# TensorE instead of DMA for the first transposes of an attention and mixture-of-experts kernel

## The chip, the core and the metric

The kernel runs on one core of a Trainium2 chip. The metric is device time in microseconds, the median of several runs. The core's engines have one queue each, worked in order: TensorE (PE in the profile; its weight loads PEld), VectorE (DVE), ScalarE (ACT), GpSimd (POOL) and SyncE (SP), which issues nearly all DMAs.

## The reference

Block-causal attention over 4 batches and 8 heads of 576 tokens, then a dense two-layer network with ELU over all 2304 tokens, then a second network with eight experts, of which every token that is not skipped takes one:

```python
def _attn_ref(q, k, v):
    scores = scale * np.matmul(q, k.transpose(0, 1, 3, 2))
    scores = np.where(block_i >= block_j, scores, -1000000000.0)   # blocks of 64
    attn = np.exp(scores - np.max(scores, axis=-1, keepdims=True))
    attn = attn / (np.sum(attn, axis=-1, keepdims=True) + 1e-09)
    return np.matmul(attn, v)
def _moe_ref(x, w_in, w_out):                    # 512 -> 2048 -> 512
    h = x @ w_in
    g = np.where(h > 0.0, h, np.exp(np.minimum(h, 0.0)) - 1.0)
    return g @ w_out
def _moe2_ref(x, w_skip, w_gate, w1, w2):        # per token: skip, or one expert
    h = np.maximum(xc[mask] @ w1[e], 0.0)
    y[mask] = gate_w[mask, None] * (h @ w2[e])
```

## The kernel before, in words

The 2304 tokens are nine chunks of 256 (`CT`). Attention feeds them: batch by batch, in groups of 64-token blocks (group 0 of batch 0 is blocks 0 to 3), for each group all four head pairs p, for each pair the blocks i. Nearly all fp32 values are carried as two fp16 halves (high and low), which are multiplied as three or so products.

- `load_raw` (L651) loads 128 tokens (tile n) of q, k or v for all heads into `raw`, a ring of three buffers.
- `prep_k` (L658) splits k into halves on ScalarE and VectorE (tile k1) and transposes them by a DMA on SyncE into KT (name kt). `prep_q` (L668) does the same with q, in two arrangements, high-low and low-high (qq, the first and second half of its first axis), of which the second takes one more ScalarE and one more VectorE instruction; one DMA transpose makes both parts of QT (qt). `prep_v` (L682) splits v with a scale from the largest value of v, which `vmax` (L613: a square with sum on ScalarE over the tile vflat) and `vscale` (L619: the maximum over partitions with two small matmuls, named bm, and a few VectorE instructions) find.
- For each pair and block, `s_unit` (L696) makes the scores in PSUM (tag s, three buffers), `x_unit` (L714) the maximum on VectorE and the exponential with its sum on ScalarE (e32, three buffers), `h_unit` (L741) the high halves of the normalised exponentials, for two blocks at a time, on ScalarE, and `l_unit` (L776) the low halves on VectorE, then a DMA transpose on SyncE from ehl into et (tag et0 to et4 by the number of 128-key tiles; et0, et1 and et3 have one buffer, et2 and et4 two). `pv` (L791) multiplies et with v's halves (xps) and copies the result into xt, the input of a chunk.
- Chunks 0 and 1 are computed in fp32. `l1` (L826) multiplies xt with the converted w_in (twi), `l1a` makes the ELU (g), `l2` (L871) multiplies with the converted w_out (two). Each of 32 raw weight tiles (rw) is loaded by `raw_load` (L454) and put in its final form by three VectorE instructions in `conv` (L480); two make one f of the eight of a layer. Chunk 0 needs the attention of group 0 for all pairs; chunk 1 needs the rest of batch 0's blocks up to 7.
- From chunk 2 on both layers are fp16 matmuls with split weights; after the last chunk come the experts.

The order. The code doesn't issue instructions at once: `Recorder` (L32) records steps with their reads, writes and buffer rings, and `order` (L149) plays the program with priced steps (`cost`, L310, and fixed latencies LAT): at each point the engine that can begin first takes, among the steps that are ready, the one recorded first. The result is each engine's queue. Group 0 of batch 0 and what it needs are recorded with an advance of 300 places (`hot`, L1147, `rc.base`). A step can be given an earliest time in `rc.ready`. Attention is recorded by place: the scores of a unit at its place x, maximum and exponential at x+1, high halves at x+2, low halves and transpose at x+3, pv five places after the last unit. So the scores of later units stand between the steps of one unit.

In the trace nearly all recorded instructions have line L307 (the recording helper), so tiles tell them apart.

Of the kernel before, what the change touches and what calls it, by code (L numbers as in the profile page):

```python
# [9 lines left out]
F32 = mybir.dt.float32  # L10
F16 = mybir.dt.float16
BF16 = mybir.dt.bfloat16
I32 = mybir.dt.int32
AF = mybir.ActivationFunctionType
# [6 lines left out]
ET_BUFS = 1, 1, 2, 1, 2  # L21
# [246 lines left out]
def _count(ap):  # L268
    n = 1
    for _, c in ap:  # L270
        n *= c
    return n
# [15 lines left out]
class _Engine:  # L288
# [21 lines left out]
    def cost(self, op, k):  # L310
        e = self.e
        out = k["out"]
        if e == "sp":
            b = _count(out.ap) * mybir.dt.size(out.dtype)
            if op == "dma_start_transpose":
                return max(1.2, b / 290e3 + 0.35), b / 290e3
            run = min(a.ap[-1][1] * mybir.dt.size(a.dtype) for a in (out, k["in_"]))
            return 0.48, b / 360e3 * (2 if run < 512 else 1)
        n = _count(out.ap[1:])
        sb = all(x.space == bass.MemoryType.SB for x in (out, k.get("in_", out), k.get("in0", out)))  # L320
        if e == "pe":
            if op == "transpose":
                return 0.2, 0.0
            t = n / 2400.0 * (4 if k["lhsT"].dtype == F32 else 1)
            here = out.offset // out.ap[0][0]
            prev, self.rec.last_pe = self.rec.last_pe, here
            return (0.02 if prev == 0 and here == 64 and n < 400 else max(t, 0.01)), 0.0
        if e == "act":
            aps = any(hasattr(k.get(x), "tensor") for x in ("scale", "bias"))
            return (0.094 if sb else 0.051) + n * 0.833e-3 + 0.093 * (aps + ("accum_out" in k)), 0.0  # L330
        if e == "dve":
            if op == "tensor_reduce":
                n = _count(k["in_"].ap[1:])
            aps = any(hasattr(k.get(x), "tensor") for x in ("scalar", "scalar1", "scalar2"))
            x = 1.0
            if op in ("tensor_copy", "tensor_scalar") and sb:
                x = 0.5 if mybir.dt.size(k.get("in_", k.get("in0")).dtype) == 4 else 0.25
            return 0.069 + n * x / 960.0 + 0.061 * aps, 0.0
        if op == "indirect_dma_start":
            return 1.05, 2.0  # L340
        return 0.15, 0.0
# [3 lines left out]
def tile_kernel(ctx, tc, q, k, v, w_in, w_out, w_skip, w_gate, w1, w2, out):  # L345
    nc = tc.nc
    B, H, S, D = q.shape
# [12 lines left out]
    G = [[[0, 1, 2, 3], [4, 5, 6, 7], [8]] if b == 0 else [[0, 1, 2, 3], [4, 5, 6, 7, 8]] for b in range(B)]  # L360
# [5 lines left out]
    mo = ctx.enter_context(tc.tile_pool(name="mo", bufs=1))  # L366
    ps = ctx.enter_context(tc.tile_pool(name="ps", bufs=1, space=PSUM))

    rc = Recorder(nc)
    wp, sm, mo, ps = (rc.pool(p_) for p_ in (wp, sm, mo, ps))  # L370
# [3 lines left out]
    ident = const.tile([128, 128], F32)  # L374
# [14 lines left out]
    def newcol(n=1):  # L389
        c = ncol[0]  # L390
        ncol[0] += n
        return slice(c, c + n)
# [28 lines left out]
    def setup_consts():  # L421
        make_identity(nc, ident)
        nc.gpsimd.memset(ones16, 1.0)
        nc.gpsimd.affine_select(out=tri16, in_=ones16, pattern=[[1, 128]], compare_op=ALU.is_gt, fill=0.0, base=0, channel_multiplier=-1)
        for e in range(E):
            nc.gpsimd.memset(rev[:, e:e + 1], float(E - e))
            nc.gpsimd.memset(eR[:, e:e + 1], float(e * R))
        nc.gpsimd.iota(tokid, pattern=[[128, NT // 128]], base=-2048, channel_multiplier=1, allow_small_or_imprecise_dtypes=True)
        nc.vector.memset(carry, 0.0)

        nc.vector.memset(carry[:, 2:3], 64.0)
        for h in range(2):
            nc.gpsimd.memset(pm[64 * h:64 * h + 64, 1:2], float(h))
            nc.gpsimd.iota(pm[64 * h:64 * h + 64, 0:1], pattern=[[0, 1]], base=64, channel_multiplier=1, allow_small_or_imprecise_dtypes=True)
# [159 lines left out]

    at = ExitStack()
    ap = rc.pool(at.enter_context(tc.tile_pool(name="attn", bufs=1)))
    XT = {}

    def xt(c):
        if c not in XT:  # L600
            if c < 2:
                XT[c] = mo.tile([128, 4, CT], F32, tag="xt", bufs=3, name="xt")
            else:
                XT[c] = mo.tile([128, 4, 2, CT], F16, tag="xt", bufs=3, name="xt")
        return XT[c]

# [5 lines left out]
    def vmax(b):  # L612
        if "vmx" not in st:  # L613
            st["vmx"] = newcol(4)
        s = st["vmx"].start
        t = st.pop(("vf", b))
        rc.scalar.activation(out=t, in_=t, func=AF.Square, accum_out=col[:, s + b:s + b + 1])

    def vscale(i):  # L619
        s = st["vmx"].start  # L620
# [22 lines left out]
    KT = {}  # L643
    QT = {}
# [3 lines left out]
    def trows(n):  # L648
        return 128 if n < 4 else 64

    def load_raw(nm, b, n):  # L651
# [3 lines left out]
        rc.sync.dma_start(out=t[0:r], in_=src[b, :, n * 128:n * 128 + r, :].rearrange("h p d -> p h d"))  # L655
        RAW[nm, b, n] = t

    def prep_k(b, n):  # L658
        r = trows(n)
        raw = RAW.pop(("k", b, n))  # L660
        if n == 0:
            KT[b] = ap.tile([128, H, S], F16, tag=f"kt{b % 2}", bufs=1, name="kt")
        k1 = ap.tile([128, H, 2, D], F16, tag="k1", bufs=1, name="k1")
        rc.scalar.activation(out=k1[0:r, :, 0, :], in_=raw[0:r], func=AF.Copy, scale=0.25)
        rc.vector.scalar_tensor_tensor(out=k1[0:r, :, 1, :], in0=raw[0:r], scalar=0.25, in1=k1[0:r, :, 0, :], op0=ALU.mult, op1=ALU.subtract)
        rc.sync.dma_start_transpose(out=KT[b][:, :, n * 128:n * 128 + r], in_=k1[0:r].rearrange("p h a d -> p (h a d)"))

    def prep_q(b, n):  # L668
        r = trows(n)
        raw = RAW.pop(("q", b, n))  # L670

        qq = ap.tile([128, 2, H, 2, D], F16, tag="qq", bufs=2, name="qq")
        for a in range(2):
            rc.scalar.activation(out=qq[0:r, a, :, a, :], in_=raw[0:r], func=AF.Copy, scale=0.5)
        rc.vector.scalar_tensor_tensor(out=qq[0:r, 0, :, 1, :], in0=raw[0:r], scalar=0.5, in1=qq[0:r, 0, :, 0, :], op0=ALU.mult, op1=ALU.subtract)
        rc.vector.tensor_copy(qq[0:r, 1, :, 0, :], qq[0:r, 0, :, 1, :])
        full = n < 4
        t = ap.tile([128, 2, H, r], F16, tag="qt" if full else "qh", bufs=3 if full else 1, name="qt")
        rc.sync.dma_start_transpose(out=t.rearrange("p a h r -> p (a h) r"), in_=qq[0:r].rearrange("p e h a d -> p (e h a d)"))
        QT[b, n] = t  # L680

# [12 lines left out]
    ET = {}  # L694
# [19 lines left out]
    def x_unit(b, p, i):  # L714
        tl, parts, mx = UN[b, p, i]

        for m, t in enumerate(tl):
            rc.vector.tensor_reduce(out=mx[:, m:m + 1], in_=t, axis=AX.X, op=ALU.max, negate=True)
        bias = mx[:, 0:1]
        if len(tl) == 2:  # L720
            bias = mx[:, 2:3]
            rc.vector.tensor_tensor(out=bias, in0=mx[:, 0:1], in1=mx[:, 1:2], op=ALU.min)
        x, u = i // 2, i % 2
        if u == 0:
            SU[b, p, x] = sm.tile([128, 8], F32, tag="su", bufs=4, name="su")
        es = []
        for m, (a, e_) in enumerate(parts):
            e32 = ap.tile([128, 64 if m else 512], F32, tag=("e32", "e3x")[m], bufs=(3, 2)[m], name="e32")
            es.append(e32[:, 0:e_ - a])
            rc.scalar.activation(out=es[m], in_=tl[m], func=AF.Exp, bias=bias, accum_out=SU[b, p, x][:, u + 2 * m:u + 2 * m + 1])  # L730
        UN[b, p, i] = es
# [5 lines left out]
    def pair(i):  # L737

        return [] if i % 2 == 0 and i < 8 else [8] if i == 8 else [i - 1, i]
# [36 lines left out]
    def l_unit(b, p, i):  # L776
        us = pair(i)
        if not us:
            return
        x = i // 2  # L780
        su = SU.pop((b, p, x))
        for u in us:
            for src, dst in e_parts(b, p, u):
                rc.vector.scalar_tensor_tensor(out=dst[:, :, 1], in0=src, scalar=su[:, 6 + u % 2:7 + u % 2], in1=dst[:, :, 0], op0=ALU.mult, op1=ALU.subtract)
            UN.pop((b, p, u))
        hl = HP.pop((b, p, x))
        n, nk = hl.shape[1:3]
        et = ET[b, p, x] = ap.tile([128, n, 2 * nk, 128], F16, tag=f"et{x}", bufs=ET_BUFS[x], name="et")
        rc.sync.dma_start_transpose(out=et.rearrange("p u n c -> p (u n) c"), in_=hl.rearrange("p u n a c -> p (u n a c)"))

    def pv(b, p, g):  # L791
# [474 lines left out]
    load_raw("q", 0, 1)  # L1266
    vflat(0)
    setup_consts()
    prep_k(0, 0)
    prep_q(0, 0)  # L1270
    load_raw("v", 0, 0)
# [244 lines left out]
    for i in range(2):  # L1516
        t = wp.tile([128, 2, PW], F32, tag=f"wo{i + 4}", bufs=1, name=f"gp{i}")
# [295 lines left out]
```

## Time and profile before

| | us |
|---|---|
| median of 3 runs | 803.34 (802.21 to 807.96) |
| profiled execution | 801.38 |
| its span, first to last instruction | 799.7 |
| TensorE busy | 699.3 (87%) |
| VectorE busy | 585.4 (73%) |
| ScalarE busy | 526.9 (66%) |
| mean granted TensorE clock | 0.986 |

The span is measured by the profiler on the core; some 1.7 us of the execution lie outside it. A row of a timeline gives the start, the time until the last of its merged instructions ended, the engine, the operation with the tiles written and read, and, in brackets, the idle time ahead of it with what ended it. A row of waits says who waited for whom, in total, how often, and the longest. A matmul's duration covers its pipeline, so the durations of neighbours overlap; busy time counts overlapping time once.

### The profile page before, as it was taken

To read this page: it belongs to the slowest core of one execution; us is meant where nothing else is said; L and a number is where in the kernel's file an instruction comes from. 1 tells how busy PE (TensorE), PEld (TensorE's weight loads), DVE (VectorE), ACT (ScalarE), POOL (GpSimd) and SP (SyncE) were. 2 spreads that over 40 slices of the span, in tenths; PEclk is the share of its full clock that TensorE was granted. 3 is DMA by queue.
4 is the path that set the end of the run, shared out by engine and by line. 5 is a ranking of instruction groups with operands and counts; after the bars stand their busy time and mean duration, and the time that the engine had idled before them with its cause. 6 is when DMAs were issued, how large, how long until landed. Compare 5 with 4: busy or idle time off the path is not lost. (4 is left out here: it accounts for less than half of the span.)

```text
span 799.7 us, 18029 instructions
## 1 busy us (share of the span) xinstructions
PE 699.3 (87%) x6586; PEld 461.1 (58%) x6586; DVE 585.4 (73%) x1721; ACT 526.9 (66%) x1166; POOL 98.3 (12%) x185
## 2 busy tenths in 40 slices
PE   0349868999998998999999999999998848998995
PEld 0238524675465655556646667675766635776763
DVE  3866988887998888987789648997876513737810
ACT  4555655999896886886578537673665425868832
POOL 2000000001001100100100100101040432322112
PEclk9999999999999999999999999999999979999998
DMA  9999999976897799898276089271564699989322
GB/s 226 256 204 291 294 299 256 213 130 122 165 176 139 138 181 202 170 197 155 49 125 143 19 162 374 94 225 40 188 181 141 123 236 236 330 240 216 70 29 39
DMA packets 300437, 141.43 MB, mean 177 GB/s; under 512 B 269659, under 2 KB 277989, under 8 KB 299808
## 3 DMA queue, kind: packets, MB, share of 16 engines
q1 hardware_dynamic: 295568, 130.65, 72.7%
q0 software_dynamic: 4752, 9.33, 4.8%
q8 instruction: 60, 0.98, 0.5%
q14 instruction: 57, 0.47, 0.2%
HBM read 76.20 MB, written 13.41 MB: 112 GB/s over the span
## 5 line engine op out<-in xcount | busy, mean ns | idle before, releaser
L307 PE MATMUL h<-xt,win 128*128 128x256 f16 x1344 | 159.5, 274 | 1.4 <-DVE n L307 1.0
L307 PE MATMUL y<-wout,g 128*128 128x512 f16 x672 | 156.5, 380 | 0.0
L307 PEld LDWEIGHTS <-win 128*128 128x128 f16 x1344 | 128.2, 98 | 28.2 <-issue 5.0
L307 PEld LDWEIGHTS <-g 128*128 128x128 f16 x672 | 62.4, 98 | 70.6 <-issue 5.2
L307 ACT ACTIVATE ehl<-e,su 128x64 f16<-128x64 f32 (+4 forms) x208 | 86.2, 470 | 22.7 <-DVE su L307 9.1
L307 ACT ACTIVATE e<-s,mx 128x64 f32<-128x64 f32 (+7 forms) x160 | 78.5, 492 | 34.0 <-DVE mx L307 16.3
L307 DVE SCALAR_TENSOR_TENSOR ehl<-e,su,ehl 128x64 f16<-128x64 f32 (+4 forms) x208 | 85.9, 442 | 9.8 <-ACT ehl L307 9.4
L307 PE MATMUL s<-kt,qt 128*64 128x512 f16 (+7 forms) x640 | 64.7, 306 | 25.6 <-ACT e L307 14.6
L307 DVE TENSOR_REDUCE mx<-s 128x1 f32<-128x64 f32 (+7 forms) x160 | 70.1, 448 | 11.5 <-PE s L307 11.1
L307 PE MATMUL xps<-et,vt 128*64 128x128 f16 (+1 forms) x1440 | 49.7, 220 | 22.0 <-DMA et<-ehl 19.0
L307 POOL MEMSET ehl<- 128x128 f16 x80 | 16.3, 210 | 403.2 <-DMA et<-ehl 284.2
L307 PEld LDWEIGHTS <-vt 128*64 128x64 f16 x1440 | 41.5, 115 | 39.3 <-issue 23.2
L307 PE MATMUL h<-xt,twi 128*128 128x256 f32 x256 | 63.3, 403 | 0.9 <-DVE g L307 0.9
L307 PE MATMUL y<-two,g 128*128 128x512 f32 x128 | 61.7, 613 | 2.4 <-DVE two L307 2.4
L307 PEld LDWEIGHTS <-qt 128*64 128x64 f16 x640 | 28.8, 115 | 57.8 <-issue 40.8
L307 PEld LDWEIGHTS h<-xt,twi 128*128 128x128 f32 x256 | 50.1, 201 | 10.6 <-DVE g L307 1.3
L307 ACT ACTIVATE el<-h,col 128x512 f32<-128x512 f32 x56 | 38.2, 682 | 25.3 <-PE h L307 25.1
L307 PE MATMUL y<-p,hh 128*128 128x512 f16 x192 | 46.0, 393 | 9.5 <-ACT hh L307 9.1
L307 ACT ACTIVATE g<-el,col 128x512 f16<-128x512 f32 x56 | 40.1, 717 | 19.6 <-DVE el L307 19.4
L307 PEld LDWEIGHTS <-hh 128*128 128x128 f16 x288 | 27.7, 99 | 43.1 <-ACT hh L307 9.6
L1450 DVE SCALAR_TENSOR_TENSOR p<-p,n,p 128x1024 f16<-128x1024 f32 x37 | 47.3, 1282 | 5.1 <-ACT p L1449 5.0
L307 PEld LDWEIGHTS <-p 128*128 128x128 f16 x768 | 45.8, 98 | 8.2 <-issue 3.7
(209 smaller groups left out, 1176.1 us busy)
## 6 DMA issues: line engine op xcount, KB each, us to landing
p<-in_moe_w_dram SPq DMA_DIRECT2D x45, 512.0 KB, 6.6
rw<-in_moe_w_in_dram SPq DMA_DIRECT2D x16, 512.0 KB, 5.1
rw<-in_moe_w_out_dram SPq DMA_DIRECT2D x16, 512.0 KB, 7.4
pb<-in_moe_w_dram SPq DMA_DIRECT2D x14, 512.0 KB, 5.6
vflat<-in_v_dram SPq DMA_DIRECT2D x4, 1152.0 KB, 7.3
out_dram<-pay SPq DMA_DIRECT2D x18, 256.0 KB, 3.5
pay_d<-pay SPq DMA_DIRECT2D x18, 256.0 KB, 2.6
raw<-in_k_dram SPq DMA_DIRECT2D x16, 256.0 KB, 3.9
```

What stands on the lines that cost most here:

```text
L307: rec.call(e, time, lambda: getattr(self.real, op)(*args, **kw), reads, writes, dma)
L1450: rc.call("dve", 1.2, lambda: nc.vector.scalar_tensor_tensor(out=half(1), in0=raw.t, scalar=sc, in1=half(0), op0=ALU.mult, op1=ALU.subtrac ...
```

## The change

For tiles 0 and 1 of batch 0 (`early`), k and q are transposed by TensorE into PSUM, in fp16, and copied from there into KT and QT: by VectorE for k, by ScalarE for q. q's second arrangement is made by transposing the halves in the other order, so that the instructions that built it for these tiles go. For group 0 of batch 0 the normalised exponentials go the same way, copied by ScalarE for even pairs and by VectorE for odd ones; odd pairs use the rings et4 and et2. The exponentials of blocks 2 and 3 of batch 0 go into a ring named el, otherwise free at that time. The square of `vmax` gets an earliest time of 11.5 in the planner. The planner prices an fp16 transpose at 0.06. GpSimd copies the identity to fp16 once. All other transposes stay DMAs.

```diff
@@ cost
             if op == "transpose":
-                return 0.2, 0.0
+                return (0.2 if out.dtype == F32 else 0.06), 0.0
@@ vmax
         rc.scalar.activation(out=t, in_=t, func=AF.Square, accum_out=col[:, s + b:s + b + 1])
+        if b == 0:
+            rc.ready[len(rc.steps) - 1] = 11.5
@@ new
+    def early(b, n):
+        return b == 0 and n < 2
+
+    def turn(out, ins, tag, dve=False):
+        t = ps.tile([128, len(ins), 128], F16, tag=tag, bufs=2, name="tp")
+        for x, a in enumerate(ins):
+            if isinstance(a, tuple):
+                for h in range(2):
+                    rc.tensor.transpose(out=t[64 * h:64 * h + 64, x, :], in_=a[h], identity=ident16)
+            else:
+                rc.tensor.transpose(out=t[:, x, :], in_=a, identity=ident16)
+        if dve:
+            rc.vector.tensor_copy(out, t)
+        else:
+            rc.scalar.activation(out=out, in_=t, func=AF.Copy)
@@ prep_k
+        if early(b, n):
+            turn(KT[b][:, :, n * 128:n * 128 + r], [k1[0:r, h].rearrange("p a d -> p (a d)") for h in range(H)], "y", True)
+            return
         rc.sync.dma_start_transpose(out=KT[b][:, :, n * 128:n * 128 + r], in_=k1[0:r].rearrange("p h a d -> p (h a d)"))
@@ prep_q
-        for a in range(2):
+        for a in range(1 if early(b, n) else 2):
             rc.scalar.activation(out=qq[0:r, a, :, a, :], in_=raw[0:r], func=AF.Copy, scale=0.5)
         rc.vector.scalar_tensor_tensor(out=qq[0:r, 0, :, 1, :], in0=raw[0:r], scalar=0.5, in1=qq[0:r, 0, :, 0, :], op0=ALU.mult, op1=ALU.subtract)
+        if early(b, n):
+            turn(t[:, 0], [qq[:, 0, h].rearrange("p a d -> p (a d)") for h in range(H)], "h")
+            turn(t[:, 1], [(qq[:, 0, h, 1], qq[:, 0, h, 0]) for h in range(H)], "h")
+            QT[b, n] = t
+            return
         rc.vector.tensor_copy(qq[0:r, 1, :, 0, :], qq[0:r, 0, :, 1, :])
@@ x_unit
+            if b == 0 and i in (2, 3):
+                e32 = mo.tile([128, 512], F32, tag="el", bufs=2, name="e32")
+            else:
+                e32 = ap.tile([128, 64 if m else 512], F32, tag=("e32", "e3x")[m], bufs=(3, 2)[m], name="e32")
@@ l_unit
-        et = ET[b, p, x] = ap.tile([128, n, 2 * nk, 128], F16, tag=f"et{x}", bufs=ET_BUFS[x], name="et")
+        y = (4, 2)[x] if b == 0 and x < 2 and p % 2 else x
+        et = ET[b, p, x] = ap.tile([128, n, 2 * nk, 128], F16, tag=f"et{y}", bufs=ET_BUFS[y], name="et")
+        if b == 0 and i in G[0][0]:
+            hf = hl.rearrange("p u n a c -> p (u n a) c")
+            turn(et.rearrange("p u n c -> p (u n) c"), [hf[:, y] for y in range(2 * n * nk)], "h", p % 2 == 1)
+            return
         rc.sync.dma_start_transpose(out=et.rearrange("p u n c -> p (u n) c"), in_=hl.rearrange("p u n a c -> p (u n a c)"))
@@ setup
     setup_consts()
+    rc.gpsimd.tensor_copy(out=ident16, in_=ident)
```

## Rows read from the trace of the kernel before

**Rows 1.** Busy time by stage; columns as its first line says (x: instructions).

```profile
core 0: us, PE busy (x) PEld busy (x) DVE busy (x) ACT busy (x) POOL busy (x), PEclk, DMA share, GB/s
0.00:55.00 55.00, 13.48 (x151) 9.32 (x151) 35.83 (x110) 29.48 (x81) 4.83 (x41) 1.00 1.08 227
22.83:54.99 32.16, 12.21 (x136) 8.66 (x137) 26.10 (x79) 20.29 (x63) 0.00 (x0) 1.00 1.10 226
55.00:92.00 37.00, 34.80 (x162) 27.80 (x161) 27.51 (x58) 24.25 (x43) 0.20 (x1) 1.00 1.08 292
92.00:144.00 52.00, 42.38 (x263) 18.88 (x263) 45.48 (x109) 29.29 (x64) 1.44 (x7) 1.00 1.09 269
150.00:640.00 490.00, 469.88 (x4520) 306.56 (x4515) 400.32 (x1271) 347.32 (x796) 51.07 (x104) 0.99 0.71 153
```

**Rows 2.** Timeline of PE, 0 to 160 us: start, us, what, idle before.

```profile
13.77 0.53 PE L307 MATMUL s<-kt,qt 128*64 128x64 f16 x8
...
22.83 1.39 PE L307 MATMUL s<-kt,qt 128*64 128x192 f16 x12 [8.17 <-DMA qt<-qq]
...
54.99 16.76 PE L307 MATMUL h<-xt,twi 128*128 128x256 f32 x64
...
145.54 1.36 PE L307 MATMUL xps<-et,vt 128*64 128x128 f16 x42
```

**Rows 3.** Waits, 0 to 60 us: in total, times, longest.

```profile
PE bm L307 <- ACT vflat L307: 13.3, 1, 13.3
...
PE s L307 <- DMA qt<-qq: 10.7, 2, 8.2
PE xps L307 <- DMA et<-ehl: 10.6, 5, 2.9
```

**Rows 4.** Timeline of SyncE's DMA queue, 0 to 60 us.

```profile
7.12 4.44 SPq L307 DMA_TRANSPOSE qt<-qq  x1
11.60 0.58 SPq L307 DMA_DIRECT2D raw<-in_q_dram  x1
...
17.29 3.38 SPq L307 DMA_TRANSPOSE qt<-qq  x1
```

**Rows 5.** Timeline of PE, 636 to 670 us.

```profile
640.23 5.53 PE L307 MATMUL hp<-mxwo,p 128*128 128x128 f16 x96 [0.87 <-ACTq L1674]
```

**Rows 6.** Groups by shape, whole span: busy, mean ns, idle before.

```profile
L307 DVE TENSOR_REDUCE mx<-s 128x1 f32<-128x512 f32 x32 | 21.6, 679 | 0.0
...
L307 DVE TENSOR_REDUCE mx<-s 128x1 f32<-128x256 f32 x16 | 6.7, 416 | 0.3 <-PE s L307 0.3
...
L307 ACT ACTIVATE pay<-y 128x512 f32<-128x512 f32 x4 | 2.4, 590 | 0.0
...
L307 ACT ACTIVATE xt<-xps 128x256 f16<-128x256 f32 x4 | 1.5, 378 | 3.0 <-PE h L307 2.5 <-PE xps L307 0.4
```

**Rows 7.** Groups by shape, 0 to 60 us: busy, mean ns, idle before.

```profile
L307 DVE SCALAR_TENSOR_TENSOR twi<-rw,twi 128x512 int32<-128x512 int32 x16 | 10.9, 686 | 0.1
...
L307 ACT ACTIVATE qq<-raw 128x512 f16<-128x512 f32 x6 | 3.4, 621 | 0.7 <-DMA raw<-in_q_dram 0.6
L307 DVE TENSOR_SCALAR twi<-rw 128x512 int32<-128x512 int32 x8 | 3.4, 420 | 1.1 <-DMA rw<-in_moe_w_in_dram 1.1
...
L307 ACT ACTIVATE vflat<-vflat 128x2304 f32<-128x2304 f32 x1 | 2.1, 2122 | 4.4 <-DMA vflat<-in_v_dram 4.4
L307 DVE SCALAR_TENSOR_TENSOR qq<-raw,qq 128x512 f16<-128x512 f32 x3 | 2.1, 688 | 1.0 <-ACT qq L307 1.0
...
L307 DVE COPY qq<-qq 128x512 f16<-128x512 f16 x3 | 0.9, 291 | 0.1
```

**Rows 8.** Timeline of DVE, 4.5 to 14 us.

```profile
4.82 0.69 DVE L307 SCALAR_TENSOR_TENSOR k<-raw,k 128x512 f16<-128x512 f32 x1 [2.15 <-ACT k L307]
```

**Rows 9.** DMA issues, 0 to 60 us: KB each, median us to landing.

```profile
raw<-in_q_dram SPq DMA_DIRECT2D x4, 256.0 KB, 4.3
...
et<-ehl SPq DMA_TRANSPOSE x8, 4.2
```

**Rows 10.** Waits of DVE, 60 to 160 us.

```profile
DVE two L307 <- DMA rw<-in_moe_w_out_dram: 5.7, 5, 2.4
...
DVE twi L307 <- DMA rw<-in_moe_w_in_dram: 3.2, 2, 2.3
```

More of the change, by code (lines that the diff above doesn't have):

```diff
@@ L596, in tile_kernel @@
     ap = rc.pool(at.enter_context(tc.tile_pool(name="attn", bufs=1)))
+    ident16 = ap.tile([128, 128], F16, tag="id16", bufs=1, name="id16")
     XT = {}
@@ L672, in prep_q @@
         qq = ap.tile([128, 2, H, 2, D], F16, tag="qq", bufs=2, name="qq")
-        for a in range(2):
+        full = n < 4
+        t = ap.tile([128, 2, H, r], F16, tag="qt" if full else "qh", bufs=3 if full else 1, name="qt")
+        for a in range(1 if early(b, n) else 2):
             rc.scalar.activation(out=qq[0:r, a, :, a, :], in_=raw[0:r], func=AF.Copy, scale=0.5)
         rc.vector.scalar_tensor_tensor(out=qq[0:r, 0, :, 1, :], in0=raw[0:r], scalar=0.5, in1=qq[0:r, 0, :, 0, :], op0=ALU.mult, op1=ALU.subtract)
+        if early(b, n):
[3 more added lines that the diff above has]
+            return
         rc.vector.tensor_copy(qq[0:r, 1, :, 0, :], qq[0:r, 0, :, 1, :])
-        full = n < 4
-        t = ap.tile([128, 2, H, r], F16, tag="qt" if full else "qh", bufs=3 if full else 1, name="qt")
         rc.sync.dma_start_transpose(out=t.rearrange("p a h r -> p (a h) r"), in_=qq[0:r].rearrange("p e h a d -> p (e h a d)"))
@@ L727, in x_unit @@
         for m, (a, e_) in enumerate(parts):
-            e32 = ap.tile([128, 64 if m else 512], F32, tag=("e32", "e3x")[m], bufs=(3, 2)[m], name="e32")
+            if b == 0 and i in (2, 3):
+                e32 = mo.tile([128, 512], F32, tag="el", bufs=2, name="e32")
+            else:
+                e32 = ap.tile([128, 64 if m else 512], F32, tag=("e32", "e3x")[m], bufs=(3, 2)[m], name="e32")
             es.append(e32[:, 0:e_ - a])
```

## The prediction

> **What bounds the kernel now.** I read the busy time by stage first, then who waited for whom in the first 60 us, then the order of TensorE's matmuls and of SyncE's issues there, and last the durations of the kinds of instruction that the change adds or removes.
>
> The stages [rows 1]: until 55 us TensorE is busy 13.5 us of 55; from 55 to 92 it is busy 34.8 of 37; from 92 to 144, 42.4 of 52 while VectorE is busy 45.5 of 52 (87%); from 150 to 640, 469.9 of 490 (96%). So the first 55 us are a stretch of waiting before TensorE, the bound of all that follows, gets its work. Its first large work is the first layer of token chunk 0 (h<-xt,twi), which begins at 54.99 [rows 2]. This needs the attention of blocks 0 to 3 of batch 0 for all four head pairs. So the question is what sets 54.99, and whether a shift of it lives on.
>
> What sets it [rows 3]: in 0 to 60 us the matmuls of s wait 10.7 us for the DMA transposes that make qt (8.2 of them in one wait), and those of xps 10.6 us in five waits for the ones that make et. The first s ran at 13.77, the first s of the second 128 tokens at 22.83 [rows 2]. Between lies SyncE's queue [rows 4]: the load of q's second tile is issued only at 11.60, behind the transpose of qq that held the queue from 7.12 for 4.44 us, and its own transpose goes out at 17.29 and takes 3.38 us to issue.
>
> **The change part by part.** Twelve DMA transposes go: kt and qt of tiles 0 and 1, and et of two shapes for four pairs. TensorE gets 2x8 transposes for k, 2x(8+16) for q, 4x(4+8) for the exponentials: 112. No 128-column fp16 transpose stands in the trace; the nearest are the matmuls with 128x128 weights and 128 columns, 96 in 5.53 us, 0.058 us each, weight loads hidden [rows 5]. The whole is 6.5 us. The first 64 sit where TensorE is idle anyway. Were they four times as long, the 24 of one q tile would put some 4 us on the start; at nothing they would save 1.4.
>
> Evictions from PSUM. On ScalarE a plain copy of 256 columns took 0.378 us and of 512 0.590 [rows 6], so 0.21 per 256 and 1.03 for 1024. On VectorE no copy out of PSUM is shown; reductions out of PSUM took 0.416 for 256 and 0.679 for 512 [rows 6], so 0.68 for 512 and 1.20 for 1024. From below the bound is the fp16 copy within SBUF, 0.291 for 512 [rows 7], 0.5 for 1024; I take 1.20, since the reductions read the memory that the copy reads. VectorE gains 2x1.20 for k and 2x(0.68+1.20) for the exponentials of the odd pairs, and loses two copies of 0.29: +5.6 us (+2.0 from below). ScalarE gains 4x1.03 for q and 2x(0.59+1.03) for the even pairs, and loses two conversions of 0.62: +6.1 us.
>
> One rule bears on the size. The Trainium skill (VectorE: DVE Perf Modes, "Why PSUM operands drop a tier") allows a copy with a PSUM operand up to twice the basic rate, and only fp32 the basic one; an fp16 copy of 1024 would then be an estimated 0.6 us, VectorE's gain 2.5 us, and the sum below some 1.5 us better. No row here shows an fp16 read of PSUM.
>
> The start. The raw tiles have three buffers, so q's second load waits until VectorE is done with the first k tile (4.82+0.69=5.5 [rows 8]) and no longer for two transposes. It goes out at 5.6 and lands 4.3 us later [rows 9], 9.9. Then ScalarE 0.62 and VectorE 0.69 [rows 7], 11.2; eight transposes 0.46; eviction 1.03, while the other sixteen run; second eviction, 13.9; s at 14. The square of vflat (2.12 us [rows 7]) is told to be due at 11.5 and may stand in ScalarE's queue before these evictions; the other end is 16.5. I take 15 against 22.83: 7.8 us gained. With the square moved, ScalarE no longer meets it before the second k tile; the wait for its sum (13.3 us, alone in the first 14 us [rows 3]) held no s. v's split, which the first xps needs, comes some 2 us behind the square; the first et needs maximum, exponential, split, transpose and eviction after its s and is later than that.
>
> The four pairs. From 22.83 to 54.99 is 32.2 us, with VectorE busy 26.1 and ScalarE 20.3 [rows 1]. Six conversions of weights lie in it, each three instructions, on average (10.9+3.4)/8=1.8 us [rows 7]: 10.8 us that can move. Each of the eight et transposes is 4.2 us from issue to landing [rows 9]; in its place stand 0.23 or 0.46 us of transposes and 0.6 to 1.2 of eviction, so 2.5 to 3.5 us less per hand-over, of which only the 10.6 us that TensorE waited can be won. What is late next is VectorE: 26.1 less 10.8 is 15.3, with the odd pairs' evictions 3.8 it is 19.1 without any conversion, and ScalarE 20.3+3.2=23.5. Some of either (the first units of blocks 4 and 5, the tiles that they need) can wait until later. The ends: 22 us (all conversions pushed out, ScalarE nearly full) and 32 (conversions stay between). I take 27, which wins half of the waits for et, 5.2 us. Chunk 0 begins at 15+27=42 instead of 55: 13 us.
>
> et gets two more buffers for odd pairs, and the exponentials of units 2 and 3 a ring of their own; both only take waits away, and I price them at nothing beyond the 27. GpSimd's copy of the identity stands behind 4.8 us of its own work, all it has before 55 [rows 1]; it may come a microsecond after the first k tile, which the 15 leaves room for. The et evictions take the PSUM buffers named h, which chunk 0 first needs after the last of them.
>
> What is given back. In front of 55 eight conversions were done, by 42 it will be about five; the first layer eats two per 4.2 us of TensorE (16.8 us for four f [rows 2]). From 55 to 144 VectorE was busy 27.5+45.5=73.0 of 89 [rows 1]; with three conversions more, 78.4 of 89, 88%, which is the share it reached in 92 to 144 while TensorE waited for it. So the length of this stretch should nearly hold. Ends: nothing, or three conversions and VectorE's new 5.6 us in full, 11. I take 3, a little over a quarter. DMA doesn't tighten it: the removed transposes carry 3.1 MB (two of 0.26, two of 0.52, four each of 0.13 and 0.26), 14 us at the 227 GB/s of that stretch [rows 1]. SyncE loses twelve issues and keeps the loads that stood behind them, and these only come sooner.
>
> A rule speaks against this change: the Trainium skill (Advanced Engine Details and Errata, "X-Bar Transpose (TRN2)") says that transpose DMAs are as fast as regular ones, 350 to 400 GB/s. At that rate an estimated 8 us of DMA time would be freed. The rows speak of latency, 4.2 us per et, not of rate, and the sum is the same by either.
>
> After 144 the shift is carried: 96% of TensorE's time from 150 to 640 is busy [rows 1], and weight loads there follow freed buffers, not a clock.
>
> **Sum.** 55 to 42 is -13, given back 3: -10 us. The profiled execution took 801.38 (span 799.7 and 1.7 around it): 791.4. It lies 2.0 under the median of 803.34, so for a median I say 793.3. A measurement tells about 1% (8 us) from no change.
>
> **Rivals.** (a) VectorE takes it back: the conversions missing at 42 and the evictions stand in front of TensorE in full, 11 of 13: 801.3. For it: 87% busy in 92 to 144, TensorE at 82%. Against: VectorE idle 19 us before 55.
> (b) The second half of the hand-over doesn't move. Chunk 1 needs blocks 4 to 7, whose last xps ran at 145.54 [rows 2]; their transposes stay DMAs behind the same queue. If they don't move at all, chunk 1 starts where it did, 803; if half as far as chunk 0, 6.5 us earlier. Between the two: 800. Against: those units stand in the queues by readiness, and their inputs come sooner too.
> (c) Everything runs free: VectorE waited 3.2 and 5.7 us for raw weights from 60 to 160 [rows 10]; with loads sooner these go, nothing is given back, and the pairs take 25: -15 less another 4: 784.
> (d) Slower: the hand-overs become serial. TensorE works in order, so a transpose that waits for VectorE's split holds the s of the next unit, and that holds maximum, exponential and split. All engine work of the pairs is 12.2+15.3+20.3, and 2.8+3.8+3.2 new: 57.6 us, run with (12.2+26.1+20.3)/32.2=1.8 engines at once before. It decides at 57.6/40=1.44 engines: below that chunk 0 starts after 55. At 1.3 it starts at 15+44.3=59.3, and with the 3 given back the time is 803.34+7.3=810.6. Against: s has three buffers, and the written order puts units apart.
> (e) That it doesn't do what it says: the planner prices a transpose at 0.06 and could put one where it waits; this is (d) in small.
>
> **How the numbers follow.** Chances: forecast 0.52 (own range 788 to 798), (a) 0.16, (b) 0.10, (c) 0.15, (d) with (e) 0.07. Faster by over 1%, below 795.3: (c) and nine tenths of the forecast, 0.62. Slower, above 811.4: half of (d), and what a reordered later stage could add, 0.06; within 1%: 0.32. The range takes (c) at its lower end and (a) and (b) whole: 783 to 802.
>
> **What would show it.** Right: s of 192 columns at 14 to 17; no DMA between ehl and et before the first h; the first h<-xt,twi at 38 to 46; the end of its stretch near 134; waits of xps in the first 45 us below 5 us. Wrong: first h after 50 ((d)), or waits for two on VectorE doubled from 92 to 144 with the first h at 42 ((a)).

## The result, and the profile after

The median is 793.14 us (789.65 to 796.98) against 802.78 for the kernel before, measured beside it: a ratio of 0.9865, 95% interval 0.9823 to 0.9908. So the change makes the kernel 1.3% faster, 9.6 us where 10 were forecast. The profiled execution after is the shortest of the four, 789.65 us, with a span of 787.9 (before 799.7), so the two profiles differ by 11.7 us where the medians differ by 9.6. The same kernel measured a second time gave 0.9867 (0.9825 to 0.9909).

The way there is another than the prediction's. First the stages. This is the busy time by stage of the kernel after: to the first layer of chunk 0, to the end of chunk 0's second layer, to the first layer of chunk 1, to the end of chunk 1's second layer, and the long stretch of [rows 1].

```profile
core 0: us, PE busy (x) PEld busy (x) DVE busy (x) ACT busy (x) POOL busy (x), PEclk, DMA share, GB/s
0.00:46.59 46.59, 25.06 (x258) 17.79 (x258) 35.65 (x108) 34.60 (x82) 5.12 (x42) 0.87 1.05 270
46.59:121.47 74.88, 71.01 (x363) 42.95 (x361) 68.99 (x153) 44.54 (x93) 1.56 (x6) 0.99 1.05 264
121.47:136.89 15.42, 8.26 (x142) 5.55 (x143) 14.80 (x74) 15.17 (x35) 0.41 (x2) 1.00 1.16 202
136.89:214.46 77.57, 77.44 (x594) 46.63 (x592) 64.11 (x195) 70.04 (x171) 6.20 (x18) 0.98 0.79 147
150.00:640.00 490.00, 466.31 (x4518) 305.50 (x4517) 388.82 (x1230) 338.36 (x768) 53.63 (x104) 0.99 0.71 153
```

And the same stages of the kernel before:

```profile
0.00:54.99 54.99, 13.47 (x150) 9.31 (x151) 35.82 (x110) 29.48 (x81) 4.83 (x41) 1.00 1.08 227
54.99:144.10 89.11, 77.29 (x426) 46.72 (x425) 73.10 (x166) 53.64 (x106) 1.65 (x8) 1.00 1.09 279
144.10:150.20 6.10, 4.66 (x94) 3.53 (x92) 6.10 (x40) 6.10 (x15) 0.20 (x1) 0.92 1.20 187
150.20:226.00 75.80, 75.61 (x571) 46.43 (x571) 65.73 (x208) 70.24 (x172) 6.35 (x18) 0.98 0.80 155
```

Read the second column, the length. The first stage is 8.4 us shorter, the second 14.2 shorter, the third 9.3 longer: 13.3 in all when chunk 1 begins. From then on TensorE is busy nearly without a gap in both kernels, and most of the shift is carried: 11.5 us at the end of chunk 1's second layer (226.0 to 214.5) and 11.8 in the span. Read the third column, TensorE's busy time, as a balance: up to chunk 1 it is 95.4 us before and 104.3 after, 8.9 more (the new transposes take 13.1, all else 4.2 less), while its idle time falls from 54.8 to 32.6, 22.2 less. 22.2 less 8.9 is the 13.3.

The timeline of TensorE in the kernel after, with the lines that answer to [rows 2]:

```profile
15.81 2.02 PE L307 MATMUL tp<-id,qq 128*128 128x128 f16 x24 [1.31 <-DVE qq L307]
...
18.47 0.37 PE L307 MATMUL s<-kt,qt 128*64 128x192 f16 x2
19.48 1.22 PE L307 MATMUL s<-kt,qt 128*64 128x192 f16 x10 [0.64 <-ACT qt L307]
...
46.59 4.68 PE L307 MATMUL h<-xt,twi 128*128 128x256 f32 x16
...
51.60 7.17 PE L307 MATMUL h<-xt,twi 128*128 128x256 f32 x32
...
117.77 3.70 PE L307 MATMUL y<-two,g 128*128 128x512 f32 x8
...
132.02 1.39 PE L307 MATMUL xps<-et,vt 128*64 128x128 f16 x42 [0.52 <-DVE col L307]
...
136.58 0.46 PE L307 MATMUL lp<-wgs,x2t 128*128 128x9 f16 x12 [1.96 <-DMA x2t<-pay]
136.89 3.35 PE L307 MATMUL h<-xt,twi 128*128 128x256 f32 x8
```

The s of the second 128 tokens runs in two parts: two of its matmuls at 18.47, the rest at 19.48, when ScalarE has copied the second part of qt. The last line is chunk 1's first layer. It stands 4.9 us behind the last xps of blocks 4 to 7 (before: 145.54 [rows 2] and 150.20, 4.7). Not all of these 4.9 us belong to the blocks. The last copy into chunk 1's xt ends at 134.67 on ScalarE, but the line above stands ahead of chunk 1 in TensorE's queue: lp, the matmuls that choose the experts for chunk 0's tokens, which wait 1.96 us for a DMA transpose of chunk 0's output (x2t). In the kernel before no lp stands ahead of chunk 1. Chunk 0 is done at 121.47, the end of the row of 117.77, and for the 15.4 us until chunk 1 TensorE has only small matmuls, 8.3 us of them.

The waits of TensorE in 0 to 60 us of the kernel after, which answer to [rows 3]:

```profile
PE tp L307 <- DVE k L307: 5.4, 1, 5.4
...
PE tp L307 <- ACT ehl L307: 3.5, 4, 2.0
...
PE xps L307 <- ACT et L307: 1.7, 1, 1.7
...
PE s L307 <- DMA qt<-qq: 1.4, 1, 1.4
...
PE xps L307 <- DVE et L307: 1.1, 1, 1.1
...
PE s L307 <- ACT e L307: 0.7, 2, 0.5
```

The 10.7 us of s for qt have become 1.4, and the 10.6 of xps for the DMAs of et are gone; in their place xps waits 2.8 us for the copies and the transposes (tp) 3.5 for the high halves and 0.6 for the low ones. And the waits of VectorE for raw weights in 60 to 160 us, which answer to [rows 10]:

```profile
DVE twi L307 <- DMA rw<-in_moe_w_in_dram: 3.0, 2, 1.6
DVE two L307 <- DMA rw<-in_moe_w_out_dram: 0.2, 1, 0.2
```

Where it waited 5.7 us for w_out, it waits 0.2. The loads go out sooner, as the timeline of SyncE's queue shows:

```profile
3.72 0.98 SPq L307 DMA_DIRECT2D rw<-in_moe_w_in_dram  x2
5.36 0.37 SPq L307 DMA_DIRECT2D raw<-in_q_dram  x1
...
11.92 2.37 SPq L307 DMA_DIRECT2D rw<-in_moe_w_in_dram  x3
...
27.38 1.33 SPq L307 DMA_TRANSPOSE kt<-k  x1
```

Five loads of weights (rw) are issued by 14.3 us, where before the first two went at 12.85. By 55 us twelve have gone against eight, and the last of all at 109.72 against 134.10. The first DMA transpose is at 27.38. In the kernel before, the twelve that are gone held the queue for 22.7 us between 5 and 51.

### The profile page after: what moved, and what is told of

Read it like the earlier page. It is cut to its first block, busy times and chain, and to the rows that moved or that the text cites. A ratio compares the mean times of both kernels' runs of the same rounds, so it can differ in the third digit from the quotient of the medians.

```text
span 787.9 us, 18237 instructions
## 1 busy us (share of the span) xinstructions
PE 713.2 (91%) x6698; PEld 472.6 (60%) x6698; DVE 586.4 (74%) x1725; ACT 532.3 (68%) x1172; POOL 99.7 (13%) x186
## 5 line engine op out<-in xcount | busy, mean ns | idle before, releaser
L307 ACT ACTIVATE e<-s,mx 128x64 f32<-128x64 f32 (+7 forms) x160 | 78.5, 493 | 23.6 <-DVE mx L307 10.7
L307 DVE TENSOR_REDUCE mx<-s 128x1 f32<-128x64 f32 (+7 forms) x160 | 70.5, 449 | 14.1 <-PE s L307 13.7
L307 PE MATMUL s<-kt,qt 128*64 128x512 f16 (+7 forms) x640 | 62.9, 305 | 7.6 <-ACT e L307 4.3
L307 ACT ACTIVATE el<-h,col 128x512 f32<-128x512 f32 x56 | 38.2, 683 | 25.8 <-PE h L307 25.3
L307 PEld LDWEIGHTS h<-xt,twi 128*128 128x128 f32 x256 | 48.4, 195 | 11.7 <-DVE g L307 2.7
L307 PEld LDWEIGHTS <-p 128*128 128x128 f16 x768 | 48.1, 101 | 7.0 <-issue 2.7
L307 PE MATMUL y<-p,hh 128*128 128x512 f16 x192 | 46.6, 397 | 6.1 <-ACT hh L307 5.7
```

What stands on the lines that cost most here:

```text
L307: rec.call(e, time, lambda: getattr(self.real, op)(*args, **kw), reads, writes, dma)
```

## Experiments

The theory: the shorter chain to chunk 0 is worth something only together with SyncE's freed queue, and what reaches the end is chunk 1's start. Its rivals: the two halves of the change simply add; the early weights alone do it; SyncE's time in issuing, or the bytes, are the cause. All marks are from each kernel's profiled execution (us); the ratios are to the kernel before run beside it. Those runs of before had medians from 802.8 to 806.2, so marks of different kernels compare to a few us only: after and after_again are one kernel, and their marks differ by 1.1 to 2.4 us, their spans by 6.7 (787.9 and 794.6).

| kernel | s 192 | chunk 0 begins | chunk 0 ends | chunk 1 begins | ratio (95%) |
|---|---|---|---|---|---|
| before | 22.8 | 55.0 | 144.1 | 150.2 | 1 |
| after | 18.5 | 46.6 | 121.5 | 136.9 | 0.9865 (0.9823, 0.9908) |
| after_again | 20.0 | 47.7 | 123.8 | 138.9 | 0.9867 (0.9825, 0.9909) |
| kq_only | 18.7 | 47.4 | 145.3 | 153.0 | 1.0005 (0.9977, 1.0032) |
| et_only | 24.3 | 53.7 | 135.2 | 149.3 | 1.0006 (0.9975, 1.0036) |
| loads_late | 17.6 | 47.1 | 138.3 | 144.4 | 0.9858 (0.9817, 0.9899) |
| g1_early | 19.6 | 47.4 | 131.5 | 142.5 | 0.9905 (0.9863, 0.9946) |
| dummies | 19.2 | 50.2 | 149.8 | 156.3 | 1.0098 (1.0067, 1.0129) |
| no_rings | 18.6 | 56.8 | 128.7 | 146.2 | 0.9931 (0.9881, 0.9980) |
| before_loads | 25.1 | 56.4 | 136.7 | 150.5 | 1.0039 (1.0011, 1.0068) |
| small_dummies | 18.0 | 44.8 | 140.3 | 145.1 | 0.9929 (0.9904, 0.9955) |
| pool_copies | 24.0 | 55.6 | 131.3 | 147.3 | 0.9972 (0.9941, 1.0004) |
| more_tiles | 19.5 | 52.1 | 130.5 | 149.6 | 1.0019 (0.9993, 1.0046) |
| square_late | 21.1 | 49.0 | 124.1 | 143.7 | 0.9912 (0.9885, 0.9939) |

One warning for all of them: each edit makes the planner write another order, so no kernel differs from another by its edit alone.

**One half at a time.** kq_only leaves the exponentials with the DMA, et_only k and q.

```diff
kq_only
-        if b == 0 and i in G[0][0]:
+        if False:
et_only
-        return b == 0 and n < 2
+        return False
```

> k and q of tiles 0 and 1 go through TensorE, the eight et transposes of group 0 stay DMAs. Theory (the two halves add up: the start from k and q, the pairs from et): the second tile's s begins at 18 to 20 as in the changed kernel, the pairs take 32 us as before, the first h of chunk 0 comes at 50 to 52, the time is 797 to 800. Rival (SyncE's queue decides: freed of the first four transposes it issues the raw weights from 4 us on, and that makes chunk 0 short): first h at 50 to 52 too, but chunk 0's two layers take 75 to 80 us instead of 89, and the time is 793 to 796.

> Only the exponentials of group 0 go through TensorE; k and q of tiles 0 and 1 stay DMA transposes. Theory (halves add): second tile's s at 22 to 24 as before, pairs 27 us, first h at 49 to 51, time 796 to 799. Rival (SyncE's queue decides): raw weights come as late as before, from 12.9 us, chunk 0's two layers take 85 us or more, time 799 to 802.

Neither half gains anything: 1.0005 and 1.0006, where both together give 0.9865. Neither expectation of either run came true. kq_only begins chunk 0 at 47.4, as early as the whole change and sooner than both sides said, and its chunk 0 takes 97.9 us where the rival said 75 to 80. TensorE and VectorE in kq_only, the waits from 47 to 153 us and from 60 to 160:

```profile
PE s L307 <- ACT e L307: 6.1, 2, 5.9
PE y L307 <- DVE two L307: 6.1, 4, 3.1
...
PE h L307 <- DVE twi L307: 2.9, 3, 1.7
```

```profile
DVE two L307 <- DMA rw<-in_moe_w_out_dram: 4.3, 6, 1.5
DVE twi L307 <- DMA rw<-in_moe_w_in_dram: 4.2, 4, 1.9
```

Chunk 0 stands 9.0 us for converted weights (y for two, h for twi), and they for their loads: from 17.8 to 45.4 us, in which seven of the eight transposes of et go through SyncE, kq_only issues no load of weights. With et_only the start stays late (24.3), chunk 0 begins at 53.7 (the theory said 49 to 51), and chunk 1 stands where it did. So the halves do not add.

**Nothing changed, and rings.** after_again is the kernel after once more. no_rings takes the extra buffers back.

```diff
-        y = (4, 2)[x] if b == 0 and x < 2 and p % 2 else x
+        y = x
-            if b == 0 and i in (2, 3):
+            if False:
```

> The changed kernel as it is, beside the other three on one chip, as their reference. The ratio to the kernel before is 0.983 to 0.990; chunk 1's first h is at 135 to 139.

> The changed kernel without the extra rings: et of odd pairs in et0 and et1, the exponentials of blocks 2 and 3 in e32. Theory (they were priced at nothing): within 0.4% of the changed kernel on this chip, first h of chunk 0 within 1.5 us of 46.6. Rival (single buffers make each pair wait for the matmuls of the one before): first h at 50 or later, time 3 us or more above the changed kernel.

Without the rings chunk 0 begins at 56.8 instead of 47.7, later than before the change. TensorE's waits in no_rings, 18 to 57 us:

```profile
PE s L307 <- ACT e L307: 6.9, 5, 2.6
PE tp L307 <- DVE ehl L307: 5.0, 6, 2.5
PE tp L307 <- ACT ehl L307: 2.3, 2, 1.9
```

The waits for e (0.7 in the kernel after) and of the transposes for ehl (4.1) are 14.2 us together. So without the rings there is no gain in this stretch. Yet the time is 0.9931 against 0.9867, with intervals that overlap: nine microseconds at the start of chunk 0 are worth 2 to 5 at the end, if anything. That is the clearest sign that chunk 0's start is not what the end hangs on.

**The queue.** dummies adds, behind each of the new turns, a DMA transpose of the same source into a tile that nobody reads: fourteen for the old twelve, since each of q's two is made in halves. small_dummies issues as many, of 128 columns each; pool_copies copies the same bytes, plain, from GpSimd's queue.

```diff
dummies (behind every turn; q twice)
+        rc.sync.dma_start_transpose(out=st["dum"][:, nd[0] % 2, 0:n], in_=src)
small_dummies
+        rc.sync.dma_start_transpose(out=st["dum"][:, nd[0] % 2, 0:1], in_=src[:, 0:128])
pool_copies
+        rc.gpsimd.dma_start(out=st["dum"][:, nd[0] % 2, 0:n].rearrange("p n c -> p (n c)"), in_=src)
```

> The changed kernel, and SyncE also issues twelve DMA transposes of the old sizes (q's in two halves) into a buffer that nobody reads. Theory (what counts is that SyncE's queue and the DMA engines are rid of the twelve, so that weight loads and the inputs of blocks 4 to 7 come sooner): first h of chunk 0 stays at 46 to 49, but chunk 1's first h goes back to 145 to 152 and the ratio to before is 0.996 to 1.004. Rival (what counts is the latency of the transposes in the chain to chunk 0): ratio 0.984 to 0.990, chunk 1's first h at 135 to 140.

> As with the twelve unread DMA transposes, but each moves only 128 columns (32 KB, half a megabyte in all instead of 3.1). Theory (SyncE's queue: the issue of a transpose and the wait for its input hold back the loads behind it, however few bytes it moves): seven or eight raw weight loads are issued by 50 us instead of eleven, chunk 1's first h is at 145 or later, ratio to before 0.996 to 1.010. Rival (the bytes in the DMA engines): ratio 0.984 to 0.991, chunk 1's first h at 136 to 141.

> The same twelve transfers with all their bytes, but as plain copies that GpSimd issues, unread as before; SyncE's queue is that of the changed kernel. Theory (SyncE's queue): ratio 0.984 to 0.991, chunk 1's first h at 136 to 141. Rival (bytes in the DMA engines): ratio 0.996 or more, weight loads land later, chunk 1's first h at 145 or later.

dummies loses the whole gain and more: 1.0098, 18.5 us over after_again on the median (814.8 less 796.32). No result waits for these transposes, and the chain to chunk 0 still runs through TensorE (50.2). What they take is SyncE's time (27.3 us in its queue, the old twelve 22.7), the DMA engines', and the source tiles until they are read (ScalarE waits 1.3 us for one). SyncE's queue in dummies:

```profile
5.48 1.41 SPq L307 DMA_TRANSPOSE dum<-k  x1
6.93 4.15 SPq L307 DMA_TRANSPOSE dum<-qq  x1
...
15.89 1.16 SPq L307 DMA_DIRECT2D rw<-in_moe_w_in_dram  x2
```

The first weights go at 15.89 as against 3.72, the last at 134.07, as in the kernel before. The Trainium skill (Advanced Engine Details and Errata, "X-Bar Transpose (TRN2)") has such transposes run at the rate of regular DMAs, 350 to 400 GB/s; by that the 3.1 MB would be an estimated 8 us of DMA time. The 18.5 us for putting them back are more, but the queue's time and the held tiles are in them, so no run here shows the rate by itself.

small_dummies has half of the gain left, 0.9929, with the last load at 127.86. Its ratio lies between the two sides, and ten weight loads are issued by 50 us, where the theory said seven or eight and the kernel after has twelve. The interval just touches that of the change, so that issues without their bytes cost something is likely and not shown.

pool_copies has less left, 0.9972, though SyncE is free of the transposes: its ratio and chunk 1's begin are the ones that the rival named. But its copies took more than the DMA engines. ScalarE in pool_copies:

```profile
12.66 0.63 ACT L307 ACTIVATE k<-raw 128x512 f16<-128x512 f32 x1 [6.63 <-DMA dum<-k]
```

The tile of k's halves (k1) has one buffer, so the second k is split only when the unread copy has left it; in the kernel after this runs at 6.46 (before at 13.04, in dummies at 12.37). That makes the start late (s at 24.0, chunk 0 at 55.6). Loads were slower too: in the first 30 us a raw weight tile landed 10.3 us after its issue, in the kernel after 6.6 (medians). Chunk 0 then takes 75.6 us, as short as in the kernel after. So with the issues in SyncE's queue chunk 0 is long (99.6 in dummies, 95.5 in small_dummies), and with copies from another queue the start is late. How much of dummies' loss is the queue's, the bytes' and the held tiles' is not separated.

**The weights' early loads.** loads_late gives the first ten raw loads about the times of the kernel before; before_loads is the kernel before with its first four loads put ahead of k and q.

```diff
loads_late
         rc.sync.dma_start(out=dst, in_=src)
+        if x < 10:
+            rc.ready[len(rc.steps) - 1] = (13, 14, 22, 23, 25, 34, 45, 48, 56, 57)[x]
before_loads
     vflat(0)
+    load_to(4)
     setup_consts()
...
-    load_to(4)
```

> The changed kernel, with the first ten raw weight loads given earliest times in the planner that are the issue times before (13 to 57 us). Theory (the early loads made chunk 0 short, but chunk 1 is held by the attention of blocks 4 to 7): chunk 0's layers take 83 us or more instead of 75, and chunk 1's first h moves from 136.9 by less than 4 us; time 793 to 797. Rival (chunk 0's length has nothing to do with the loads): 74 to 77 us, and the time is that of the changed kernel, 792 to 794. Third (loads carry most of the whole gain): time 798 or more.

> The kernel before, with the first four raw weight loads recorded ahead of the k and q transposes. Theory (SyncE's queue counts, but its transposes remain): chunk 0 still begins at 53 to 57, the ratio is 0.996 to 1.003. Rival (early weight loads alone make chunk 0 short): chunk 0's layers take 82 us or less, ratio 0.990 to 0.995.

loads_late is a miss for the idea that early weights make the gain: chunk 0 takes 91.2 us again, as before the change, and the ratio is 0.9858, the same as the change's. Chunk 1 begins 7.5 us later than in the kernel after, where the theory allowed 4. Nor did VectorE wait for the late weights: 3.6 us for raw tiles until chunk 1, in the kernel after 3.8, before 10.0. In before_loads chunk 0 takes 80.3 instead of 89.1, and nothing is gained: chunk 1 begins at 150.5, and the ratio is 1.0039. So chunk 0 is short in the orders with early weights, and chunk 0's length is not what the end hangs on either.

**Blocks 4 to 7.** If chunk 1's attention sets the end, it might be put earlier in the record.

```diff
-(frac - 0.5) / 0.491
+(frac - 0.3) / 0.6
```

> The changed kernel, with the units of blocks 4 to 7 recorded from 0.3 of chunk 0 on instead of 0.5. Theory (chunk 1 waits for these units, 121.5 to 136.9, and they can come earlier): chunk 1's first h at 126 to 132, time 784 to 790. Rival (VectorE's total work up to there is the bound, so what comes earlier pushes conversions back): the second layer of chunk 0 ends 4 us or more later than 121.5, chunk 1 begins at 134 to 138, time 791 to 796.

It wasn't: chunk 0 ends at 131.5 instead of 121.5, chunk 1 begins at 142.5, and the ratio is 0.9905. The work of blocks 4 to 7 was put in chunk 0's way. In the third stage of the kernel after VectorE is busy 14.8 of 15.4 us and ScalarE 15.2; an earlier place adds no room on them.

**Further.** more_tiles transposes tiles 2 and 3 on TensorE too, with the PSUM buffers named y in place of h for their q; square_late lets the square of vflat wait until 17.

```diff
more_tiles
-        return b == 0 and n < 2
+        return b == 0 and n < 4
...
+            turn(t[:, 0], [...], "h" if n < 2 else "y")
+            turn(t[:, 1], [...], "h" if n < 2 else "y")
square_late
-            rc.ready[len(rc.steps) - 1] = 11.5
+            rc.ready[len(rc.steps) - 1] = 17.0
```

> The changed kernel with k and q of tiles 2 and 3 of batch 0 transposed by TensorE too, so four more DMA transposes leave SyncE's queue before 70 us. Theory (SyncE's queue holds chunk 1): chunk 1's first h at 128 to 135, ratio 0.976 to 0.984, 2 to 8 us below the changed kernel. Rival (VectorE and ScalarE, 87% busy and more until there, are the bound now): ratio 0.985 to 0.992.

> The changed kernel with the earliest time of the square at 17 instead of 11.5. Theory (the square stands before q's second tile on ScalarE, and that put the start at 18.5 instead of 15; but the start of chunk 0 isn't what sets the end): s of 192 columns at 15 to 17, ratio within 0.4% of the changed kernel's 0.987. Rival (the start counts in full): first h 2 us or more earlier and ratio 0.980 to 0.984. Third (v's split and the first xps come late instead): first h at 48 or later.

more_tiles loses the whole gain, 1.0019, with chunk 0 at 52.1 and chunk 1 at 149.6. Fewer DMA transposes still, and no gain: "the fewer the better" is not the rule. Why this extension costs so much was not settled. square_late doesn't bring the start forward (21.1) and gives 0.9912; the reason stands in the next section. No version was better than the change.

**Taken together**, sort the table by chunk 1's begin: the kernels that gain 0.9% or more stand at 137 to 144, those of 0.7% at 145 and 146, 0.3% at 147, the rest from 149 on. Sorted by chunk 0's begin they don't order (47.4 for a ratio of 1.0005, 56.8 for 0.9931), nor by chunk 0's end (128.7 for 0.9931, 130.5 for 1.0019). The order by chunk 1 is rough: loads_late, with the lowest ratio, stands at 144.4, and from chunk 1's begin to the end of the span the profiles take 649 to 659 us (before 649.5, after 651.0, et_only 659.3).

The stages show which engine has the work until chunk 1. Add up the fourth column, VectorE: 115.0 us before and 119.4 after, and 115 to 123 in every kernel of the table. What differs is its idle time: 35.2 us before, 17.5 after, 33.1 in kq_only, 30.8 in et_only, 37.5 in dummies. In the kernel after VectorE is busy 87% of the time until chunk 1 begins, TensorE 76%. No run takes work from VectorE there, so whether it now sets chunk 1's begin is untested.

## Why the prediction was right, step by step

The time was right, the way to it was not: the sum was -13 and +3, and the profile shows -8.4, -14.2 and +9.3. Steps failed on both sides and cancelled, which is luck.

**The start (term -7.8): mis-sized, 3.4 to 4.4.** The s came at 18.5 and 19.5 instead of 15, beyond the mark of 14 to 17. (The prediction's own steps add up to 13.7, not 13.9, which changes nothing.) The load of q's second tile was issued at 5.36, where 5.6 was forecast. What failed is "lands 4.3 us later". The issues at 4 to 7 us of the kernel after, with KB and median us to landing:

```profile
rw<-in_moe_w_in_dram SPq DMA_DIRECT2D x2, 512.0 KB, 6.9
raw<-in_q_dram SPq DMA_DIRECT2D x1, 256.0 KB, 8.0
```

It took 8.0 us, to 13.4. In front of it stood 1.15 MB of vflat, issued at 2.80, and 1 MB of weights, issued at 3.72. That the loads "only come sooner" was so; that they would be issued ahead of q, whose load then takes 8.0 us instead of 4.3, was left out. The other half is the square, which stands in ScalarE's queue ahead of the conversion of q and ends at 13.36, so that q is converted at 13.79, behind one more step (ehl). Two experiments bear on this. ScalarE in loads_late, where no weights go before 10.46:

```profile
13.33 0.20 ACT L307 ACTIVATION_READ_ACCUMULATOR vflat<-vflat 128x1 f32 x1
13.42 0.62 ACT L307 ACTIVATE qq<-raw 128x512 f16<-128x512 f32 x1
```

And in square_late:

```profile
14.57 0.63 ACT L307 ACTIVATE qq<-raw 128x512 f16<-128x512 f32 x1 [0.52 <-DMA raw<-in_q_dram]
17.59 1.02 ACT L307 ACTIVATE qt<-tp 128x1024 f16<-128x1024 f16 x1 [2.39 <-PE tp L307]
18.51 2.12 ACT L307 ACTIVATE vflat<-vflat 128x2304 f32<-128x2304 f32 x1
...
20.62 1.01 ACT L307 ACTIVATE qt<-tp 128x1024 f16<-128x1024 f16 x1
```

Without the weights in front q is there when the square ends at 13.4; how much sooner it landed is not shown. Without the square in front ScalarE waits for the load itself, to 14.57. Either is enough to make q late, so taking one away brings little (17.6) or, where the late square falls between the two copies of qt, harm (21.1).

**The four pairs (27 us): the number right, its source not.** It was 27.1, from 19.48 to 46.59, so the begin of chunk 0 at 46.6, past the mark of 38 to 46, is late by the start's error alone. No DMA for et stands before it, and xps waits 3.6 us in the first 45, as the marks said. But the term was to come from et's hand-overs, 5.2 us of the 10.6. In their place stand 2.8 us of xps for the copies and 4.1 of the transposes for ehl, so 3.7 were won there. More came from a wait that the prediction did not name, in the kernel before, 0 to 60 us:

```profile
PE s L307 <- ACT e L307: 6.7, 5, 2.2
```

It is 0.7 in the kernel after, 6.9 in no_rings: this is what the rings took away. From the first s of 192 columns to chunk 0 the kernel before takes 32.2 us, the one after 28.1, kq_only, with the rings and et's DMAs, 28.7 (with 3.5 us less of weight conversions on VectorE in it), no_rings 38.2. So "I price them at nothing", of the rings, was the wrong step, and that the whole came to 27 was luck. The single prices were off in both directions. The groups that the change added, in the kernel after, 0 to 60 us:

```profile
L307 PE MATMUL tp<-id,ehl 128*128 128x128 f16 x48 | 7.0, 288 | 4.5 <-ACT ehl L307 3.5 <-DVE ehl L307 0.6
L307 ACT ACTIVATE qt<-tp 128x1024 f16<-128x1024 f16 x4 | 4.1, 1021 | 2.8 <-PE tp L307 2.8
...
L307 DVE COPY et<-tp 128x1024 f16<-128x1024 f16 x2 | 1.4, 688 | 0.3 <-PE tp L307 0.3
L307 ACT ACTIVATE et<-tp 128x512 f16<-128x512 f16 x2 | 1.2, 596 | 0.0
L307 DVE COPY et<-tp 128x512 f16<-128x512 f16 x2 | 0.8, 411 | 0.0
```

ScalarE's copies were priced at 1.03 and 0.59 and took 1.02 and 0.60. VectorE's were priced at 1.20 and 0.68 and took 0.69 and 0.41, so the reductions of [rows 6] were the wrong neighbour. By the Trainium skill (VectorE: DVE Perf Modes, "Why PSUM operands drop a tier") the estimate for 1024 was 0.6; the trace agrees with it rather than with the term. A row of 24 transposes takes 2.0 us, 0.08 each, not 0.058.

**What is given back (+3): wrong in sign.** "The length of this stretch should nearly hold" failed: it went from 89.1 to 74.9, and its end came at 121.5, not 134. The step counted conversions on VectorE and took the supply of raw weights as no limit. TensorE's idle time in the stretch fell from 11.8 us to 3.9; its waits of y for two (2.4) went, and so did those of s for e (5.2), of which the weights are no part. The other 6.3 of the 14.2 us is TensorE's work, 77.3 us before and 71.0 after: 12 matmuls of s, 42 of xps and 9 of cn (column sums of weights) now run after chunk 0, 4.5 us with overlaps, and the same 128 of h and 64 of y show 2.4 us less. Rival (c) had the right place, "with loads sooner these go".

**"After 144 the shift is carried": it failed at the hand-over to chunk 1.** Of the 22.6 us by which chunk 0 ended sooner, 9.3 were lost before chunk 1: TensorE works 3.6 us more there (8.26 and 4.66) and is idle 5.7 more, 2.0 of which are the wait of lp for x2t, the rest waits of s, cn, bm and xps, none over 1.8 us in sum. This is rival (b), whose price was 800, and its mechanism was right for the most part: in every kernel measured chunk 1 begins 1.8 to 5.3 us behind the last xps of these blocks. What it missed is that these blocks came sooner too, by 13.5 us (145.54 to 132.02); that they "stand in the queues by readiness, and their inputs come sooner too" was the argument against it. From chunk 1 on the shift is carried but for some 2 us, as forecast.

**The rest.** (a) took VectorE for the next limit: chunk 0 leaves it 92% busy (69.0 of 74.9) and the stage behind it 96%, but chunk 0 did not grow by it. (d) and (e) did not happen: chunk 0 begins 8.4 us earlier.

What is shown: with SyncE's queue (and the source tiles) taken up again, the gain is gone, although the chain keeps its TensorE transposes; each half alone is worth nothing; the kernels that begin chunk 1 earlier are by and large the faster ones. What stays open: what in the order puts the last of blocks 4 to 7 where it is. loads_late, with late weights and a long chunk 0, gains as much as the change, so the way from the freed queue to chunk 1's begin does not go through chunk 0's weights; that the inputs and transposes of blocks 4 to 7 pass a shorter queue is argued and not shown. The traces give it a small part at most: kt and qt of tiles 2 and 3 are issued at 27.4, 37.2, 41.2 and 48.7 us, before at 32.7, 36.1, 47.0 and 50.8, while xps of the four pairs of these blocks come 4.9, 8.7, 10.9 and 13.5 us sooner. The lead grows in the stretch in which VectorE's idle time falls from 16.0 us to 5.9.

## What to carry to other kernels

Find the last hand-over behind which the bound engine runs without a gap (here chunk 1's first layer) and price a change by what moves that, not by the first wait that it removes. When DMAs leave a queue, go through what stood behind them: the loads that now go earlier can stand ahead of the next urgent one (here it took 8.0 us instead of 4.3). Price the buffers that go with a change, too: here chunk 0 began nine microseconds later without them. Measure halves together as well as apart: two parts that relieve the same queue need not show anything alone. And an unread copy put in as a test holds its source tile, which can be what it measures.

## What the runs showed of the hardware that was not expected

A DMA transpose costs the queue that issues it, whoever reads the result: in the kernel before, twelve held SyncE 22.7 us, from 1.2 to 4.4 each. Fourteen that nobody read held it 27.3 us in dummies, and with a fraction of the bytes (32 KB each) still 18.9 in small_dummies, none below 1.09.

The granted clock of TensorE fell while it was doing more than before. The kernel after, in stretches of 3 us (the clock stands behind the five busy times):

```profile
29.00:32.00 3.00, 0.86 (x6) 0.44 (x7) 3.00 (x8) 3.00 (x9) 0.00 (x0) 0.92 1.13 269
32.00:35.00 3.00, 2.62 (x31) 2.22 (x32) 2.87 (x10) 3.00 (x11) 0.00 (x0) 0.51 1.11 239
35.00:38.00 3.00, 1.34 (x14) 0.85 (x14) 3.00 (x10) 3.00 (x12) 0.00 (x0) 1.00 1.09 417
```

0.50 is the level of 1.2 GHz; in the 3 us in which it began to fall TensorE was busy 0.86 us. It was back at 1.00 from 35 to 38, then at 0.50 to 0.56 until 47. In the kernel before the clock was 1.00 all the way to 55 us with TensorE busy 13.5 us of 55 [rows 1]. The first 16 matmuls of h took 4.68 us, 32 at the full clock 7.17, so about a microsecond went there. The clock in this stretch is not the same from kernel to kernel (18 to 47 us: 0.50 in no_rings, 0.79 in the kernel after, 1.00 in small_dummies), nor from one execution of a kernel to the next (0.50 in after_again). Part of the 1.1 to 2.4 us between the marks of after and after_again may be this; it was not measured apart.
